# Chunk sizes of the first MLP: six chunks of up to 448 tokens in place of eight of 256 and 320

## The chip, the cores and the metric

The kernel runs on one core of a Trainium2 chip. TensorE (PE) multiplies, VectorE (DVE), ScalarE (ACT) and GpSimd (POOL) do the elementwise work, and the SyncE queue (SP) issues most transfers. Each engine takes its own instructions in order. The metric is the device time of one launch in microseconds; the program computes all of the reference in that launch.

## The reference

Sliding-window attention with 8 heads, then two gated MLPs, all in float32:

```
scores = (q @ k.T) / sqrt(64) - slope[h] * |i - j|      # 4 batches, 8 heads, 576 positions, 64 wide
scores = where(0 <= i - j < 128, scores, -1e9);  attn = softmax(scores);  x = attn @ v
x = x as (2304 tokens, 512)
x = max(max(x @ w1, x @ w2), x @ w3) @ w_out            # first MLP, 768 wide
out = (silu(x @ w_gate) * (x @ w_val)) @ w_out2         # second MLP, 1536 wide
```

## The kernel before

Float32 products are made of three fast matmuls each: a value is split into a rounded head and a remainder, and `mm3` (L124 to L129) adds head by head, head by remainder and remainder by head. The splitting is elementwise work: ACT copies (L112, L276, L285), DVE and POOL subtract (L90, `low`).

**Attention.** A unit (`Unit`, L289) is one block of 128 queries (64 at the end of a batch) of one pair of heads; there are 80. It has four steps: `st_scores` (two to four matmuls, then mask, bias and minimum on DVE at L319 and L324, exp on ACT at L329), `st_normalise`, `st_transpose` (two PE transposes at L361, split, two selects on POOL at L377) and `st_values` (probability times value, L391 or L405, and the split of the result into the MLP's input tile `x`). The steps of neighbouring units are staggered by the lags LN, LT, LV = 1, 2, 4. Units are grouped in pieces (b, s): s = 0 holds a batch's queries 0 to 255, s = 1 its queries 256 to 575. The first three pieces, (0,0), (0,1) and (1,0), are `native`: their operands aren't split, and a matmul of theirs appears as two records. For the others `prep_head` (L272) splits each head's queries and keys when a piece begins (tiles `r`, `kl`), and `prep_v` the values.

**First MLP.** A chunk is a piece's tokens: eight chunks, alternately 256 and 320. `up_groups` has 18 groups of 12 matmuls (6 blocks of the width, 3 weights); the first result is copied by ACT (L168), the other two are joined by a maximum on DVE (L170), and POOL splits the block into `h` (L93, L90). `down_groups` has 72 matmuls; ACT copies the four results to `y` (L197, two buffers) and issues the store to `y_dram` on its own queue. The results of both go through four PSUM banks (`ps_m`, L84). Scores have two banks, transposes one, probability times value one (`ps_v`, L215). The 18 weight tiles of the up products are unpacked from 64-bit words and split (`prep_up`, `single`: L101 on ACT, L104, L105, L107 and L90 on DVE), while the first pieces of attention and the first chunk run.

**Second MLP.** `second` (L502) prepares weights (`prep`: `gates`, `values`, `mixed`, `outs`) and tokens in passes of four blocks and then runs products (L621 to L623) and down products (L701 to L703) for 36 steps.

**Order.** `spread` (L487) deals the pieces of side work among the groups of the main work in program order: up(0) with the weights and the second half of piece 1, up(1) with piece 2, and so on; the last chunk is overlapped with the first 25 pieces of the second MLP's preparation (L752 to L755). A scheduler then fixes the order on each engine by its own timeline. Within it, evictions of PSUM have a high priority (HIGH).

Of the kernel before, what the change touches and what calls it, by code (L numbers as in the profile page):

```python
# [20 lines left out]
P = 128  # L21
# [3 lines left out]
SUBS = ((0, 256), (256, 320))  # L25
KEY0 = (0, 128)
KEYN = (256, 512)
BLOCKS = ((0, 1), (2, 3, 4))
# [15 lines left out]
HIGH, EARLY, LAST = 100, 3, 9  # L44
NORM = "aa"
A2, A3 = 4, 2
# [11 lines left out]
def kernel(ctx: ExitStack, tc, q0, k0, q1, k1, qk0, qk1, vv, w123, wo1, wgv, wo2, out):  # L58
# [20 lines left out]
    wraw = em("wraw", 2)  # L79
    hp = em("hp", 2 * NF1)  # L80
    xp = em("xp")
    tmp = em("tmp", 2)
    dram = en("dram", space=bass.MemoryType.DRAM)
    ps_m = en("ps_m", 4, space=PSUM)  # L84
# [63 lines left out]
    def prep_down(k):  # L148
        wo[k] = down_tile(f"wo_{k}")
        for i in range(2):  # L150
            src = wo1[k * P:(k + 1) * P, i * 256:i * 256 + 256]
            raw = words(src, wraw, "wr", 256) if i else words(src, tmp, "y", 256)
            prep_w(raw, wo[k][:, :, i * 256:i * 256 + 256], rest=nc.gpsimd)

    def up_groups(b, s):

        n = SUBS[s][1]
        m = {}

        def group(f, e):  # L160
            xt = x_t[b, s]
# [17 lines left out]
    def down_groups(b, s):  # L179
        t0, n = SUBS[s]  # L180
        t0 += b * S

        def part(ps, d, ks):
            for k in ks:
                ht = hs[b, s, k]
                mm3(ps[:, :n], wo[k], d * P, ht[:, 0, :], ht[:, 1, :], k == 0, k == NF1 - 1)

        def group(ds):
# [13 lines left out]
    order = [(b, s) for b in range(B) for s in range(2)]  # L202
# [11 lines left out]
    ps_t = ea("ps_t", 1, space=PSUM)  # L214
    ps_v = ea("ps_v", 1, space=PSUM)  # L215
# [3 lines left out]
    fill = att.tile([P, 1, 32], F32, name="fill")[:, :, :1]  # L219
# [4 lines left out]
    def load_first(s, p):  # L224

        nq, nk = SUBS[s][1], KEYN[s]
        c0, nkb = KEY0[s] // P, nk // P
        q = hp.tile([P, 2, nq], F32, tag=f"h{s}", name="qz", bufs=NF1)
        if s == 0:
            if p % 2 == 0:  # L230
                first["k", p] = first["k", p + 1] = qkr.tile([P, 832], F32, tag="qkr", name="kn")
                first["v", p] = first["v", p + 1] = vp.tile([P, 2, 2, 2, P], F32, tag="v", name="vn", bufs=3)
            k, v = first["k", p][:, p % 2 * nk:], first["v", p][:, p % 2, 0]
        else:
            k = prep.tile([P, 832], F32, tag="r", name="kn")
            if p % 2:
                v = vp.tile([P, 4, P], F32, tag="rv", name="vn")
            else:
                v = vp.tile([P, 4, 2, P], F32, tag="v", name="vn", bufs=3)[:, :, 0]
        nc.sync.dma_start(out=k[:, :nk], in_=(k0, k1)[s][0, p])  # L240
        nc.sync.dma_start(out=q, in_=(q0, q1)[s][0, p])
        if s == 0 and p % 2 == 0:
            nc.sync.dma_start(out=first["v", p][:, :, 0], in_=vv[0, p:p + 2, :, c0:c0 + nkb].rearrange("b p k d -> p b k d"))
# [45 lines left out]
    class Unit:  # L289


        def __init__(u, b, s, p, j):
# [3 lines left out]
            u.kb = j - 1 - KEY0[s] // P  # L296
# [576 lines left out]
```

## Time and profile before

| | |
|---|---|
| median of 3 runs | 862.67 us (861.38 to 863.37) |
| the profiled execution | 863.15 us, its span 861.4 us |
| PE, weight loads, DVE, ACT, POOL busy | 98%, 92%, 68%, 49%, 44% of the span |
| mean granted clock of PE | 0.994 of full speed |
| matmuls of the first MLP | 1152 of 256 columns and 1152 of 320 |

Busy time of PE counts matmuls that overlap, so the pace of a stage is read from the starts of neighbouring matmuls in the timeline, not from their durations. A window row gives, for a stretch of the span, the busy time and number of instructions of each engine, then the granted clock, the share of the DMA engines, and GB/s.

### The profile page before, as it was taken

To read this page: it belongs to the slowest core of one execution; us is meant where nothing else is said; L and a number is where in the kernel's file an instruction comes from. 1 tells how busy PE (TensorE), PEld (TensorE's weight loads), DVE (VectorE), ACT (ScalarE), POOL (GpSimd) and SP (SyncE) were. 2 spreads that over 40 slices of the span, in tenths; PEclk is the share of its full clock that TensorE was granted. 3 is DMA by queue.
4 is the path that set the end of the run, shared out by engine and by line. 5 is a ranking of instruction groups with operands and counts; after the bars stand their busy time and mean duration, and the time that the engine had idled before them with its cause. 6 is when DMAs were issued, how large, how long until landed. Compare 5 with 4: busy or idle time off the path is not lost.

```text
span 861.4 us, 15755 instructions
## 1 busy us (share of the span) xinstructions
PE 847.5 (98%) x5352; PEld 791.9 (92%) x5352; DVE 588.4 (68%) x1551; ACT 426.0 (49%) x1182; POOL 382.2 (44%) x555
## 2 busy tenths in 40 slices
PE   8998999999999999999999999999999999999998
PEld 5687999999999999999989999999999999999996
DVE  7998956766678675646979989995564844433342
ACT  6976747847577575624446555543422422221220
POOL 5576867766777677563433231221421221211110
PEclk9998999999999999999999999999999999999999
DMA  9841614324222231302368686914939322736322
GB/s 330 308 151 57 186 44 133 92 72 129 65 73 76 94 113 34 128 2 60 138 209 296 202 309 236 327 64 138 333 138 314 123 80 74 263 128 223 132 74 97
DMA packets 59088, 130.26 MB, mean 151 GB/s; under 512 B 6272, under 2 KB 17536, under 8 KB 59008
## 3 DMA queue, kind: packets, MB, share of 16 engines
q1 hardware_dynamic: 54400, 124.54, 42.9%
q10 hardware_dynamic: 4608, 4.72, 1.6%
q8 instruction: 42, 0.69, 0.3%
q14 instruction: 38, 0.31, 0.1%
HBM read 93.85 MB, written 35.39 MB: 150 GB/s over the span
## 4 chain that ended last, share of the span: by engine, by line
PE 87%; DVE 5%; DMA 4%; ACT 1%; issue 1%; POOL 1%; SPq 0%; DVEq 0%; ACTq 0%; POOLq 0%
PE ps L128 10%; PE ps L127 10%; PE ps L129 10%; PE pg L622 7%; PE pg L623 7%; PE pg L621 7%; PE po L703 6%; PE po L702 6%; PE po L701 6%; PE pc L621 3%; PE pc L622 3%; PE pc L623 3%; PE pv L405 3%; PE pt L361 2%; PE sc L316 1%
## 5 line engine op out<-in xcount | busy, mean ns | idle before, releaser
L90 POOL TENSOR_TENSOR act<-h,act 128x384 fp32r<-128x384 f32 x72 | 80.9, 1144 | 286.1 <-ACT act L112 266.9
L129 PE MATMUL ps<-x,w 128*128 128x320 f32 (+1 forms) x576 | 173.3, 302 | 0.1
L127 PE MATMUL ps<-x,w 128*128 128x320 f32 (+1 forms) x576 | 172.8, 304 | 0.4 <-ACT w L112 0.3
L128 PE MATMUL ps<-x,w 128*128 128x320 f32 (+1 forms) x576 | 172.4, 300 | 0.0
L621 PE MATMUL pg<-ya,u 128*128 128x384 f32 x360 | 121.4, 337 | 1.8 <-ACT y L197 1.8
L622 PE MATMUL pg<-ya,u 128*128 128x384 f32 x360 | 121.6, 338 | 0.0
L623 PE MATMUL pg<-ya,u 128*128 128x384 f32 x360 | 121.2, 337 | 0.0
L127 PEld LDWEIGHTS ps<-x,w 128*128 128x128 f32 x576 | 109.0, 190 | 3.1 <-ACT w L112 1.0
L129 PEld LDWEIGHTS ps<-x,w 128*128 128x128 f32 x576 | 109.5, 190 | 2.5 <-DVE w L90 1.1
L128 PEld LDWEIGHTS ps<-x,w 128*128 128x128 f32 x576 | 109.5, 190 | 1.3 <-issue 0.9
L377 POOL TENSOR_SCALAR_AFFINE_SELECT t<-pk 128x512 fp32r<-128x512 f32 (+3 forms) x128 | 78.3, 634 | 55.2 <-PE pv L405 18.5
L702 PE MATMUL po<-u,act 128*128 128x512 f32 x216 | 85.2, 394 | 0.0
L703 PE MATMUL po<-u,act 128*128 128x512 f32 x216 | 84.6, 395 | 0.0
L701 PE MATMUL po<-u,act 128*128 128x512 f32 x216 | 83.9, 389 | 0.0
L630 DVE TENSOR_TENSOR u<-pg,s 128x384 f32<-128x384 f32 x72 | 39.6, 552 | 60.9 <-PE pg L623 60.7
L329 ACT ACTIVATE z<-z,mn 128x128 f32<-128x128 f32 (+1 forms) x160 | 63.2, 397 | 24.4 <-DVE mn L324 23.8
L621 PEld LDWEIGHTS pg<-ya,u 128*128 128x128 f32 x360 | 68.1, 189 | 6.1 <-ACT y L197 2.4
L622 PEld LDWEIGHTS pg<-ya,u 128*128 128x128 f32 x360 | 68.1, 189 | 4.1
L623 PEld LDWEIGHTS pg<-ya,u 128*128 128x128 f32 x360 | 68.0, 189 | 0.6
L170 DVE TENSOR_TENSOR m<-ps,m 128x256 f32<-128x256 f32 (+1 forms) x96 | 43.1, 450 | 26.9 <-PE ps L129 25.6
L101 ACT ACTIVATE wf<-wr 128x512 f32<-128x512 f32 (+1 forms) x66 | 41.5, 632 | 37.6 <-DMA wr<-wgv 20.9
L352 ACT ACTIVATE z<-z,rc 128x128 f32<-128x128 f32 (+1 forms) x144 | 49.8, 395 | 19.4 <-DVE rc L343 17.9
(115 smaller groups left out, 2051.4 us busy)
## 6 DMA issues: line engine op xcount, KB each, us to landing
ya<-a_dram SPq DMA_DIRECT2D x56, 384.0 KB, 4.8
a_dram<-ya SPq DMA_DIRECT2D x42, 384.0 KB, 5.7
wr<-wgv SPq DMA_DIRECT2D x24, 512.0 KB, 5.2
qkr<-qk SPq DMA_DIRECT2D x24, 416.0 KB, 3.5
wr<-w SPq DMA_DIRECT2D x18, 512.0 KB, 5.9
o_dram<-acc SPq DMA_DIRECT2D x36, 256.0 KB, 2.8
acc<-o_dram SPq DMA_DIRECT2D x36, 256.0 KB, 2.7
wr<-wo SPq DMA_DIRECT2D x12, 512.0 KB, 5.0
```

The lines of the kernel that those rows point to most:

```text
L90: eng.tensor_tensor(out=out, in0=raw, in1=head.bitcast(F32), op=ALU.subtract)
L127: nc.tensor.matmul(ps, wh, xt_h, start=first, stop=False)
L128: nc.tensor.matmul(ps, wh, xt_l, start=False, stop=False)
L129: nc.tensor.matmul(ps, wl, xt_h, start=False, stop=last)
L329: nc.scalar.activation(out=z[:m, a], in_=z[:m, a], func=AF.Exp, scale=-1.0, bias=mn[:m, a:a + 1], accum_out=sm[:m, a:a + 1],)
L377: nc.gpsimd.affine_select(out=t[:, i, :n, :, :m], in_=w[:, :n, :, :m], compare_op=op, fill=0.0, base=0, pattern=[[0, n], [0, 2], [-sign, m ...
L621: nc.tensor.matmul(o, wh, y[:, 0], start=first and k == 0, stop=False, skip_group_check=True)
L622: nc.tensor.matmul(o, wh, y[:, 1], start=False, stop=False, skip_group_check=True)
L623: nc.tensor.matmul(o, wl, y[:, 0], start=False, stop=k == 1, skip_group_check=True)
L701: nc.tensor.matmul(po, ah, w[:, 0], start=j == 0, stop=False)
L702: nc.tensor.matmul(po, ah, w[:, 1], start=False, stop=False)
L703: nc.tensor.matmul(po, al, w[:, 0], start=False, stop=j == PASS - 1)
```

## The change

The chunks of the first MLP no longer follow the pieces of attention. There are six, of 256, 320, 384, 448, 448 and 448 tokens, across the borders of batches, and the pieces are cut so that each chunk is filled by whole pieces: two in batch 0, three in batches 1, 2 and 3. `SUBS` holds them per batch as ranges of blocks, and `span` gives a piece's first query, its queries, first key and keys. Shorter pieces mean more of them: 8 that aren't native in place of 5, so `prep_head` runs 64 times in place of 40, and `prep_v` 32 times in place of 20; the first three pieces are as before. Where a piece has at most 128 queries, DVE subtracts the queries' remainder, not POOL.

The first MLP has three PSUM banks (MB) and probability times value two (VB); the four banks come back for the second MLP (`ps_m2`). `h` has one set of six buffers for the later chunks, not two; the transposed probabilities `t` have three buffers. The side work is dealt out in other shares (A2, A3, LAST), and for the first pass of the second MLP the output weights are prepared after all the others (`late`).

```diff
-SUBS = ((0, 256), (256, 320))
-KEYN = (256, 512)
-BLOCKS = ((0, 1), (2, 3, 4))
+CHUNKS = ((0, 256), (256, 320), (576, 384), (960, 448), (1408, 448), (1856, 448))
+WIDE = 448
+SUBS = (((0, 2), (2, 5)), ((0, 2), (2, 3), (3, 5)), ((0, 2), (2, 3), (3, 5)), ((0, 1), (1, 3), (3, 5)))
+ORDER = [(b, s) for b in range(4) for s in range(len(SUBS[b]))]
+NATIVE = ORDER[:3]
+def span(b, s):
+    j0, j1 = SUBS[b][s]
+    q0, k0 = j0 * 128, max(j0 - 1, 0) * 128
+    return q0, min(j1 * 128, 576) - q0, k0, j1 * 128 - k0
-HIGH, EARLY, LAST = 100, 3, 9
+HIGH, EARLY, LAST = 100, 3, 3
-A2, A3 = 4, 2
+A2, A3 = 8, 5
+QV = 128
+N1, N2 = 21, 25
+MB, TB, VB = 3, 1, 2
...
-    ps_m = en("ps_m", 4, space=PSUM)
+    ps_m = mctx.enter_context(pool("ps_m", MB, space=PSUM, side="right", reuse_waits="tile"))
...
-    def up_groups(b, s):
-        n = SUBS[s][1]
+    def up_groups(c):
+        n = CHUNKS[c][1]
...
-    ps_v = ea("ps_v", 1, space=PSUM)
+    ps_v = ea("ps_v", VB, space=PSUM)
...
-        low(nc.gpsimd, r[D:P, :nq], raw[D:P, :nq], r[D:P, :nq])
+        low(nc.vector if nq <= QV else nc.gpsimd, r[D:P, :nq], raw[D:P, :nq], r[D:P, :nq])
...
-            return [lambda: (load(0), load(1)), gates, values, lambda: (load(2), mixed()), outs]
+            return [lambda: (load(0), load(1)), gates, values, mixed, lambda: load(2), outs]
-        def preps(fs):
+        def preps(fs, late=False):
             todo = [prep(f) for f in fs]
+            if late:
+                out = todo[0][:3] + todo[1][:1]
+                for n, pieces in enumerate(todo):
+                    out += pieces[3:4]
+                    if n + 2 < len(todo):
+                        out += todo[n + 2][:1]
+                    if n + 1 < len(todo):
+                        out += todo[n + 1][1:3]
+                return out + [piece for pieces in todo for piece in pieces[4:]]
...
-    spread(up_groups(0, 1), conv_o, a2[:len(a2) * A2 // 8])
-    spread(down_groups(0, 0) + down_groups(0, 1), a2[len(a2) * A2 // 8:] + a3[:len(a3) * A3 // 8])
-    spread(up_groups(*order[2]), a3[len(a3) * A3 // 8:], early=EARLY)
-    for i in range(3, len(order) - 1):
-        spread(down_groups(*order[i - 1]) + up_groups(*order[i]), attn_units(i + 1), early=EARLY if i + 2 < len(order) else LAST)
+    a2 = attn_units(2) + attn_units(3)
+    a3 = attn_units(4) + attn_units(5)
+    spread(up_groups(1), conv_o, a2[:cut2])
+    spread(down_groups(0) + down_groups(1), a2[cut2:] + a3[:cut3])
+    spread(up_groups(2), a3[cut3:], early=EARLY)
+    spread(down_groups(2) + up_groups(3), attn_units(6) + attn_units(7) + attn_units(8), early=EARLY)
+    spread(down_groups(3) + up_groups(4), attn_units(9) + attn_units(10), early=LAST)
...
-    conv = tokens_steps(0) + preps(range(PASS))
-    spread(down_groups(*order[-2]) + up_groups(*order[-1]), conv[:21])
+    conv = tokens_steps(0) + preps(range(PASS), late=True)
+    spread(down_groups(4) + up_groups(5), conv[:N1])
```

Two places show what the scheduler makes of it. The first is DVE at the end of the first chunk, in the kernel before: `w_5_1` and `w_5_2` are the last two of the 18 weight tiles that up(0) needs, `m` is the maximum of one of its groups, `kl` and `r` are remainders of keys and queries of a piece that isn't native.

```order
L90 TENSOR_TENSOR w_5_1_1272<-wr,w_5_1_1272 128x512
L319 COPY_PREDICATED sc<-later,fill 128x2x128
L104 TENSOR_SCALAR wf<-wf 128x256
L105 SCALAR_TENSOR_TENSOR wf<-wr,wf 128x256
L343 RECIPROCAL rc<-sm 128x2
L107 SCALAR_TENSOR_TENSOR wr<-wr,wf 128x256
L90 TENSOR_TENSOR w_5_2_1336<-wr,w_5_2_1336 128x512
L170 TENSOR_TENSOR m_1313<-ps_1320,m_1313 128x256
```

The same place on DVE now, the last twelve rows up to the same tile:

```order
L336 COPY_PREDICATED sc<-later,sc 128x2x128
L105 TENSOR_TENSOR kl<-qkr,r 128x256
L105 TENSOR_TENSOR r<-qkr,r 64x128
L358 TENSOR_SCALAR sm<-sm 128x2
L105 TENSOR_TENSOR kl<-qkr,r 128x256
L105 TENSOR_TENSOR r<-qkr,r 64x128
L120 SCALAR_TENSOR_TENSOR wf<-wr,wf 128x256
L341 ISA z,mn<-sc,bias 128x128
L341 ISA mn 128x1
L341 ISA z,mn<-sc,bias 128x128
L341 ISA mn 128x1
L105 TENSOR_TENSOR w_5_2_1333<-wr,w_5_2_1333 128x512
```

Between the two tiles there were five instructions, and there are sixteen: scores of later units and key and query remainders of piece (1,1), which before came after this chunk, stand ahead of its last weight tiles.

The second place is ACT at the end of the first MLP, in the kernel before: `y_6904` to `y_6960` are the last results of the last down groups, `u0_4` to `u2_4` and `wf` belong to the second MLP's weights, `s1` is an eviction of its first product.

```order
L198 DMA y_dram_85<-y_6904 128x320
L112 CAST u0_4_6668<-wr_6614 128x512
L101 ACTIVATE wf_6963<-wr_6907 128x512
L112 CAST u1_4_6785<-wr_6732 128x512
L197 COPY y_6930<-ps2_6911 128x320
L112 CAST u2_4_6938<-wr_6850 128x512
L198 DMA y_dram_85<-y_6930 128x320
L197 COPY y_6960<-ps2_6941 128x320
L101 ACTIVATE wf_7005<-wr_6909 128x512
L644 COPY s1_6994<-pg_6987 128x384
```

The same place on ACT now:

```order
L211 COPY y_6381<-ps2_6341 128x448
L212 DMA y_dram_82<-y_6375 128x448
L127 CAST u3_2_6421<-tt_6413 128x512
L212 DMA y_dram_82<-y_6381 128x448
L211 COPY y_6410<-ps2_6391 128x448
L127 CAST u0_4_6490<-wr_6446 128x512
L212 DMA y_dram_82<-y_6410 128x448
L127 CAST u1_4_6524<-wr_6493 128x512
L127 CAST ya_6665<-yr_6578 128x384
L127 CAST ya_6668<-yr_6578 128x384
L211 COPY y_6443<-ps2_6424 128x448
L212 DMA y_dram_82<-y_6443 128x448
```

No unpacking (`wf`) of freshly loaded weights stands between the last four results any more; two casts of the next tokens (`ya`) stand before the fourth.

## Rows read from the trace of the kernel before

**Rows 1.** The page's busy time of each engine.

```profile
PE 847.5 (98%) x5352; PEld 791.9 (92%) x5352; DVE 588.4 (68%) x1551; ACT 426.0 (49%) x1182; POOL 382.2 (44%) x555
```

**Rows 2.** Window of the steady stretch: stretch, length, busy time and count by engine.

```profile
140.00:390.00 250.00, 250.00 (x1940) 247.09 (x1940) 171.64 (x635) 153.18 (x491) 170.86 (x295) 1.00 0.26 80
```

**Rows 3.** Windows of the start, as rows 2.

```profile
50.00:60.00 10.00, 10.00 (x80) 8.35 (x79) 9.14 (x26) 7.85 (x28) 8.37 (x13) 1.00 0.52 154
60.00:70.00 10.00, 9.66 (x85) 8.44 (x84) 8.90 (x24) 6.26 (x22) 8.42 (x11) 1.00 0.36 111
70.00:80.00 10.00, 7.87 (x39) 6.45 (x40) 7.75 (x27) 5.24 (x20) 5.67 (x13) 0.66 0.14 41
80.00:90.00 10.00, 9.87 (x75) 8.61 (x74) 8.80 (x24) 9.28 (x32) 4.73 (x9) 1.00 0.13 43
```

**Rows 4.** Windows of the passage to the second MLP, as rows 2.

```profile
440.00:450.00 10.00, 8.23 (x42) 7.58 (x41) 5.43 (x8) 5.98 (x12) 4.76 (x3) 0.89 0.96 304
450.00:460.00 10.00, 10.00 (x57) 10.00 (x56) 9.78 (x20) 6.00 (x12) 2.15 (x1) 0.94 0.87 276
```

**Rows 5.** PE timeline, 256 columns: start, duration, engine, line.

```profile
374.20 0.28 PE L128 MATMUL ps<-x,w 128*128 128x256 f32 x1
...
377.31 0.28 PE L127 MATMUL ps<-x,w 128*128 128x256 f32 x1
```

**Rows 6.** PE timeline, 320 columns.

```profile
418.75 0.31 PE L127 MATMUL ps<-x,w 128*128 128x320 f32 x1
...
422.57 0.31 PE L129 MATMUL ps<-x,w 128*128 128x320 f32 x1
```

**Rows 7.** PE timeline of the second MLP, 512 and 384 columns.

```profile
500.51 0.39 PE L701 MATMUL po<-u,act 128*128 128x512 f32 x1
...
501.67 0.34 PE L621 MATMUL pg<-ya,u 128*128 128x384 f32 x1
...
505.05 0.33 PE L621 MATMUL pc<-ya,u 128*128 128x384 f32 x1
...
506.96 0.33 PE L623 MATMUL pg<-ya,u 128*128 128x384 f32 x1
```

**Rows 8.** PE waits of the passage, 440 to 470 us: total, times, longest.

```profile
PE pg L621 <- ACT y L197: 1.8, 2, 1.1
```

**Rows 9.** ACT timeline of the passage; in brackets the idle time before.

```profile
444.22 0.66 ACT L101 ACTIVATE wf<-wr 128x512 f32<-128x512 f32 x1 [2.74 <-DMA wr<-wgv]
...
445.32 0.43 ACT L197 COPY y<-ps 128x320 f32<-128x320 f32 x1
...
447.30 0.42 ACT L197 COPY y<-ps 128x320 f32<-128x320 f32 x1 [0.98 <-DMA y_dram<-y]
```

**Rows 10.** DVE groups by form: count, busy us, mean ns, idle before.

```profile
L324 DVE CUSTOM_DVE_ANT_0 z<-sc,bias 128x128 f32<-128x128 f32 x128 | 32.0, 282 | 1.0
...
L319 DVE COPY_PREDICATED sc<-later,sc 128x256 f32<-128x256 int16 x48 | 20.0, 417 | 10.1 <-PE sc L316 8.0 <-PE sc L311 1.6
...
L90 DVE TENSOR_TENSOR kl<-qkr,r 128x256 fp32r<-128x256 f32 x16 | 10.1, 652 | 1.1 <-ACT r L276 1.0
```

**Rows 11.** DVE timeline at the end of the first chunk.

```profile
90.30 0.28 DVE L324 CUSTOM_DVE_ANT_0 z<-sc,bias 128x128 f32<-128x128 f32 x1
...
90.51 0.28 DVE L324 CUSTOM_DVE_ANT_0 z<-sc,bias 128x128 f32<-128x128 f32 x1
...
91.05 0.41 DVE L170 TENSOR_TENSOR m<-ps,m 128x256 f32<-128x256 f32 x1
```

**Rows 12.** PE timeline of native attention.

```profile
66.16 1.47 PE L311 MATMUL sc<-qkn 128*128 128x256 f32 x8
67.47 0.38 PE L361 MATMUL pt<-ident,z 128*128 128x128 f32 x2
...
68.76 0.28 PE L129 MATMUL ps<-x,w 128*128 128x256 f32 x1
68.97 0.67 PE L391 MATMUL pv<-t,vn 128*64 128x128 f32 x8
```

More of the change, by code (lines that the diff above doesn't have):

```diff
@@ L57, with kernel @@
 @with_exitstack
-def kernel(ctx: ExitStack, tc, q0, k0, q1, k1, qk0, qk1, vv, w123, wo1, wgv, wo2, out):
+def kernel(ctx: ExitStack, tc, q0, k0, q1, k1, *rest):
+    qks, (vv, w123, wo1, wgv, wo2, out) = rest[:-6], rest[-6:]
+    qks = dict(zip([u for u in ORDER if u not in NATIVE], qks))
     nc = tc.nc
@@ L200, in down_groups @@
         return [lambda ds=ds: group(ds) for ds in ((0, 1), (2,), (3,))]
-    order = [(b, s) for b in range(B) for s in range(2)]
     actx = ExitStack()
@@ L242, in load_first @@
         if s == 0 and p % 2 == 0:
[L243 removed]
+            nc.sync.dma_start(out=first["v", p], in_=vv[0, p:p + 2, :, c0:c0 + nkb].rearrange("b p k d -> p b k d"))
         elif s:
@@ L295, in __init__ @@
             u.k0 = P if j == 0 else 0
-            u.kb = j - 1 - KEY0[s] // P
-            u.q0 = j * P - SUBS[s][0]
+            q0, u.nq, k0, _ = span(b, s)
+            u.kb = j - 1 - k0 // P
+            u.q0 = j * P - q0
     pairs = {}
     def st_scores(u):
-        nq = SUBS[u.s][1]
+        nq = u.nq
         sc = ps_s.tile([P, 2, 256], F32, tag="sc", name="sc")
@@ L418, in x_part @@
         m = u.mq
-        n = SUBS[u.s][1]
-        if (u.b, u.s) not in x_t:
-            t = xp.tile([P, NP, 2, n], F32R, tag=f"x{u.s}", name=f"x{u.s}")
-            x_t[u.b, u.s] = [t[:, p] for p in range(NP)]
-        return x_t[u.b, u.s][u.p][:, :, u.q0:u.q0 + m]
+        t0 = u.b * S + u.j * P
+        c = max(i for i in range(len(CHUNKS)) if CHUNKS[i][0] <= t0)
+        t0 -= CHUNKS[c][0]
+        if c not in x_t:
+            t = xp.tile([P, NP, 2, CHUNKS[c][1]], F32R, tag=f"x{c % 2}", name="x")
+            x_t[c] = [t[:, p] for p in range(NP)]
+        return x_t[c][u.p][:, :, t0:t0 + m]
     def split_x(u, xr):
@@ L429, in split_x @@
         low(nc.gpsimd, xt[:, 1], xr[:, :m], xt[:, 0])
-    units = [Unit(b, s, p, j) for b, s in order for p in range(NP) for j in BLOCKS[s]]
-    todo = [(b, s, p) for b, s in order for p in range(NP)]
+    units = [Unit(b, s, p, j) for b, s in ORDER for p in range(NP) for j in range(*SUBS[b][s])]
+    todo = [(b, s, p) for b, s in ORDER for p in range(NP)]
     raws = {}
@@ L443, in prep_next @@
             b, s, p = todo[i]
-            pairs[b, s, p] = heads if native(b, s) else [prep_head(s, r) for r in heads]
-            pairs[b, s, p].append(rv if native(b, s) else prep_v(s, rv))
+            pairs[b, s, p] = heads if native(b, s) else [prep_head(b, s, r) for r in heads]
+            pairs[b, s, p].append(rv if native(b, s) else prep_v(b, s, rv))
     def begin():
@@ L553, in preps @@
                 more = todo[n + 1] if n + 1 < len(todo) else []
-                out += pieces[3:4] + more[:1] + pieces[4:] + more[1:3]
+                out += [lambda a=pieces[3], b=pieces[4]: (b(), a())] + more[:1] + pieces[5:] + more[1:3]
             return out
@@ L750 @@
     preps, keep, tokens_steps, tokens_again, head, middle, tail, down = second(apool, raws2, ps_o)
-    conv = tokens_steps(0) + preps(range(PASS))
-    spread(down_groups(*order[-2]) + up_groups(*order[-1]), conv[:21])
-    spread(down_groups(*order[-1]), conv[21:25])
-    conv = conv[25:]
+    conv = tokens_steps(0) + preps(range(PASS), late=True)
+    spread(down_groups(4) + up_groups(5), conv[:N1])
+    spread(down_groups(5), conv[N1:N2])
+    conv = conv[N2:]
     mctx.close()
+    ps_m = em("ps_m2", 4, space=PSUM)
     temp = em("temp")
@@ L847 @@
         "k1": c(kt[:1, ..., 128:640].reshape(1, NP, P, 512)),
-        "qk0": twice(np.concatenate([qt[..., 0:256], kt[..., 0:256]], axis=-1)),
-        "qk1": twice(np.concatenate([qt[..., 256:576], kt[..., 128:640]], axis=-1)),
+        **{
+            f"qk{b}{s}": twice(np.concatenate([qt[b:b + 1, ..., q:q + m], kt[b:b + 1, ..., k:k + n]], axis=-1))[0]
+            for b, s in ORDER if (b, s) not in NATIVE for q, m, k, n in [span(b, s)]
+        },
         "vv": c(vpad.reshape(B, NP, 2, 5, P, D).transpose(0, 1, 4, 3, 2, 5).reshape(B, NP, P, 5, P)),
```

97 lines of the change are left out of this document (50 added, 47 removed).

## The prediction, made before the changed kernel had run

> **What bounds the kernel now.** I read the page first: TensorE is busy 98% of the span [rows 1]. Then the windows by stage. From 140 to 390 us PE has no idle time at all, while DVE is busy 172 of 250 us, ACT 153 and POOL 171 [rows 2]; the last column but one says that the transfers take a quarter of the DMA engines. In that stretch only the time of the matmuls themselves counts, and work on the other engines is free as long as it stays within its 30 to 40% of idle time. Two places are different. In the first 90 us PE has gaps and DVE is nearly full: 9.14, 8.90, 7.75 and 8.80 of each 10 us from 50 to 90, and from 70 to 80 the granted clock falls to 0.66 after PE had stood still [rows 3]. And at the passage to the second MLP PE is idle 1.77 of the 10 us from 440, with the clock at 0.89 and 0.94 [rows 4]. So I price three things: the pace of matmuls by width, the start, the passage.
>
> **Pace.** A busy PE row overlaps its neighbours, so I take starts. 256 columns: 26 steps from 374.20 to 377.31, 0.1196 us each [rows 5]. 320: 26 steps from 418.75 to 422.57, 0.1469 [rows 6]. 384: 11 steps from 505.05 to 506.96, 0.1736; 512: 5 steps from 500.51 to 501.67, 0.232 [rows 7]. Every chunk has 216 up and 72 down matmuls, whatever its width. Before, 4 chunks of each width: 1152 x (0.1196 + 0.1469) = 307.0 us. Now 288 x (0.1196 + 0.1469 + 0.1736 + 3 x w), where w is the step of 448 columns, which no row shows. Halfway between 384 and 512 it is 0.2028, and the sum 302.0: **-5.0 us**. By the price per column of the wide rows (0.452 to 0.453 ns) w is 0.2025 to 0.2030; by that of the 320 row (0.459 ns) 0.2057, and the gain 2.5. I keep 2.5 to 5.3 and take 5.0, since the two wide rows enclose 448. The matmuls of attention are as many as before: 80 units, the same three native pieces.
>
> The Trainium skill, TensorE: Matmul & The Clock Gate, Back-to-back issue gap, gives a step of N / 2.4 ns plus about 2.5 ns. By that only the 2.5 ns of the 576 matmuls that go would be won, 1.4 us. It does not agree with the rows here: it makes 109 ns of 256 columns, where the row has 119.6 [rows 5].
>
> **The passage.** PE waited 1.8 us for `y` copies [rows 8]. The rows of ACT show why: the third copy (445.32) stood behind a `wf` (444.22) that had waited 2.74 us for a weight load, and the fourth waited for the store of an earlier `y` [rows 9]. Now no `wf` stands between the last four `y`; the output weights come after them, attention ends earlier against the end of the first MLP (its last value matmuls stand 246 us of first-MLP matmuls after the start in the order, by the steps above, not 259), so DVE has about 10 us more for the second MLP's weights, and a down group of 448 columns lasts 18 x 0.203 = 3.7 us, not 2.6, so a store has longer to free its `y`. What there is to win is 1.77 us of idle time and, at the lower clock, 10 x 0.11 + 10 x 0.06 = 1.7 [rows 4], together 3.5. I take **-3.2** and leave 0.3 for the cast of the next tokens ahead of the fourth `y`, which waits for its load. Ends: 0, if another load takes the blocking place, and -3.5.
>
> **The start.** Here the scheduler's order costs something. Counted in the order of DVE up to the last maximum of up(0) (at 91.05 before [rows 11]), there are more instructions now: 10 bias-and-minimum, 5 masks, 8 key remainders of 256 columns, 2 of 384, 8 query remainders on 64 partitions, 9 tiny ones on two columns; one key remainder of 512 and three unpackings of 256 columns fewer. Neighbours on DVE overlap by 0.07 us: an instruction of 0.28 has a successor after 0.21 [rows 11]. With durations less 0.07 [rows 10]: 10 x 0.21 = 2.1; 5 x 0.35 = 1.7; 8 x 0.58 = 4.6; 2 x 0.7 (between one and one and a half times 0.652, less the overlap) = 1.4; the 8 query remainders, an operation DVE did not do, at no more than 0.21 = 1.7; 9 x 0.12 (an estimate: about half the 0.21 of a longer one) = 1.1; less 4 x 0.58 = 2.3. Together 10.3 us more DVE work ahead of the end of the first chunk. PE has more to do up to there as well: 17 score matmuls of split pieces (256 columns, 0.12) 2.0; 2 native ones (8 records, four instructions, in 1.31 us [rows 12]) 0.7; 10 transposes, at most 0.12 each, 1.2; 10 native value matmuls (8 records, four instructions, 0.67) 1.7; six up(1) matmuls fewer, 0.9. That is 4.7, work that is only earlier, not more. If DVE is the bound, the surplus 10.3 - 4.7 = 5.6 is lost, since PE has no idle time later in which an earlier attention would pay. But DVE had 0.86 + 1.10 + 2.25 + 1.20 = 5.4 us idle from 50 to 90 [rows 3], and the second bank for values and the third buffer of `t` let units run further ahead into it. I take half of that: 5.6 - 2.7 = **+2.9**. Ends: 0.2, and 5.6 for full DVE; and 3.4 us (10 x (1 - 0.66) [rows 3]) either way for the clock, which fell after the gap there and may fall once more or not at all.
>
> PE enters native value matmuls from other work 8 times more often in the new order (42, not 34), as one now often stands alone between matmuls of the chunk. An entry has a step of 0.21 (68.76 to 68.97 [rows 12]) in place of 0.12; with the way back, which I bound by 0 and the same 0.09, 0.7 to 1.4: **+1.0**.
>
> **What costs nothing.** Splitting more pieces adds 24 casts and 12 value casts on ACT, 24 key and 24 query remainders on DVE; a part of that is in the start's sum, the rest is spread over 250 us in which DVE idles 78 and ACT 97 [rows 2]. POOL gets fewer columns of queries. Maxima and copies have fewer instructions on more columns. SP issues 24 transfers more, smaller ones, and the value and key loads of piece (1,1) now pass the last loads of the down weights, which are wanted only after up(1); a quarter of the DMA engines is in use there. Three banks for `ps_m`: an eviction may now be two groups late, not three, before PE waits: 2 x 12 x 0.12 = 2.9 us in up(0), 4.9 us with 448 columns, against 0.41 for a maximum [rows 11]. That cover is gone only if DVE or ACT has 3 us of other work queued ahead of it, as can be in the start; it belongs to the slow rival below.
>
> **Sum.** -5.0 - 3.2 + 2.9 + 1.0 = -4.3. The profiled execution took 863.15 (span 861.4), so 858.85; the median of the runs is 0.48 lower, which gives **858.4 us**.
>
> **Rivals.** (a) The start isn't slowed: DVE takes the earlier work into its idle time and the gap around 70 us with its low clock goes. For it: DVE's largest idle time lies just there, and units wait less for value banks. Against: DVE is over 88% busy in the three other windows. -5.0 - 3.2 - 3.4 + 1.0 = -10.6: 852.1. (b) The passage isn't mended: something else stands in front of a `y` (the `ya` casts wait for loads that wait for buffers). For it: the DMA share there is 0.96 [rows 4]. -5.0 + 2.9 + 1.0: 861.6. (c) Width saves only a fixed cost of the matmuls that go: 320 columns lie 0.1469 - 320 x 0.4525 = 2.1 ns above the wide rows' price, and 576 x 2.1 ns = 1.2, so -1.2 - 3.2 + 3.9 = -0.5: 862.2. The 256 column row, 3.8 ns above that price, speaks against it. This is the case that the rule of the Trainium skill, TensorE: Matmul & The Clock Gate, leads to. (d) Slower: at the end of the first chunk DVE's queue becomes what PE waits for. The surplus of 5.6 is lost in full, with three banks PE stalls on maxima behind key remainders as well, and the clock falls a second time (3.4), with 1.4 for the entries: 5.6 + 3.4 + 1.4 = 10.4 against -5.0 - 3.2: +2.2, 864.9. It decides once the start loses more than 8.2 us; for it speaks DVE's order, against it that the clock fell only once in 90 us so far.
>
> **Chances.** The forecast, taken from 855 to 860.9: 0.48. (a) 0.22. (b) 0.12 and (c) 0.06, both within 0.2%, which is 861.0 to 864.4 and about what a measurement of this kernel can tell from no change. (d) 0.12. So faster 0.70, same 0.18, slower 0.12. The range takes in (a), (b), (c) and the middle of (d): 851 to 865. The forecast's own range is 855 to 861.
>
> **What would show it.** Steps near 0.203 between matmuls of 448 columns; under 0.5 us of idle PE and a clock of 1.00 between the last down group and the first products; the last maximum of up(0) on DVE at 96 to 100 us; PE without idle time from there to the passage. I am wrong if 448 columns take 0.206 or more, if the start ends within 2 us of where it did, or if PE waits anywhere in the middle.

## The result: slower, and the profile after

The changed kernel takes **872.3 us** (median of four runs), the kernel before 862.0 beside it. One of the four, the profiled one, ran at a clock of 0.85 from end to end and took 923.5 us, so the ratio, 1.011 (95% interval 1.0077 to 1.0143), is of the other three (869.8 to 873.1), and the profile shown is of a second set. That set gave 871.31 against 862.78: 1.0102 (1.0078 to 1.0126); its profiled run has a span of 870.9 us. 858.4 was predicted, and faster.

The page's busy times of the kernel after, against [rows 1]: PE's busy time hardly differs, with 576 matmuls fewer, and its idle time is 7.8 us longer of the 9.5 by which the spans differ.

```profile
PE 849.2 (98%) x4776; PEld 775.9 (89%) x4776; DVE 601.1 (69%) x1575; ACT 430.9 (49%) x1198; POOL 380.2 (44%) x543
```

The pace, from PE's timeline of the kernel after: seven steps of 448 columns, from the first row here to the second, take 1.42 us, 0.203 each (start, duration, engine, line).

```profile
329.83 0.37 PE L142 MATMUL ps<-x,w 128*128 128x448 f32 x1
...
331.25 0.36 PE L143 MATMUL ps<-x,w 128*128 128x448 f32 x1
```

The windows of the kernel after, in the columns of [rows 3], and the steady stretch of [rows 2]. From 50 to 100 us PE is now idle 1.27 + 0.05 + 1.70 + 2.03 + 0.84 = 5.9 us, before 2.6; DVE is over 90% busy in four of the five. The granted clock is 0.83 in two windows, where it was 0.66 in one before: either way 10 us x 0.34 = 3.4 us, so the clock is no part of the difference here.

```profile
50.00:60.00 10.00, 8.73 (x68) 6.70 (x67) 9.62 (x30) 9.09 (x35) 6.80 (x11) 1.00 0.47 147
60.00:70.00 10.00, 9.95 (x75) 7.92 (x76) 8.52 (x30) 8.40 (x31) 7.66 (x17) 1.00 0.56 179
70.00:80.00 10.00, 8.30 (x63) 6.57 (x61) 9.86 (x32) 9.80 (x34) 4.42 (x9) 1.00 0.34 106
80.00:90.00 10.00, 7.97 (x44) 6.87 (x44) 9.79 (x30) 7.81 (x28) 3.98 (x6) 0.83 0.26 81
90.00:100.00 10.00, 9.16 (x57) 9.16 (x58) 9.17 (x34) 7.50 (x24) 3.03 (x5) 0.83 0.36 100
140.00:390.00 250.00, 248.07 (x1489) 233.65 (x1488) 172.91 (x630) 155.71 (x497) 165.08 (x286) 1.00 0.30 92
```

DVE's timeline of the kernel after at the last maximum of up(0), which answers to [rows 11]: it stands at 98.42, 7.4 us later, with a mask, a reciprocal and a key remainder of attention in front of it.

```profile
97.29 0.42 DVE L336 COPY_PREDICATED sc<-later,sc 128x256 f32<-128x256 int16 x1
97.62 0.16 DVE L360 RECIPROCAL rc<-sm 128x2 f32<-128x2 f32 x1
97.70 0.80 DVE L105 TENSOR_TENSOR kl<-qkr,r 128x384 fp32r<-128x384 f32 x1
98.42 0.41 DVE L185 TENSOR_TENSOR m<-ps,m 128x256 f32<-128x256 f32 x1
```

The passage, in windows of the kernel after ([rows 4]). The first MLP ends at 445.6; behind it PE is idle 2.79 and 2.13 us of 10, before 1.77 of 10 once.

```profile
440.00:450.00 10.00, 9.87 (x52) 9.14 (x51) 7.05 (x11) 5.48 (x11) 3.85 (x2) 1.00 0.75 237
450.00:460.00 10.00, 7.21 (x40) 6.57 (x40) 5.79 (x11) 3.55 (x6) 1.32 (x2) 1.00 0.30 102
460.00:470.00 10.00, 7.87 (x36) 7.55 (x36) 6.41 (x13) 4.44 (x9) 1.81 (x2) 0.83 0.95 344
```

What PE waits for there and in the end of the attention, 379 to 625 us (total, times, longest). No `y` copy is among it, as [rows 8] had it; the second MLP's own evictions have taken its place.

```profile
PE pg L649 <- ACT s L672: 2.1, 1, 2.1
PE pg L649 <- ACT h L701: 1.7, 2, 1.6
PE ps L142 <- POOL x L108: 1.6, 1, 1.6
PE pg L649 <- DVE u L658: 1.4, 2, 1.2
PE pc L649 <- DVE u L658: 1.2, 2, 0.8
PE ps L142 <- POOL h L108: 0.8, 1, 0.8
```

ACT's timeline says why ([rows 9]; in brackets the idle time before). The last two `y` copies, shown here, wait for nothing but PE and for the casts of the next tokens ahead of the fourth. But two `wf`, for output weights, hold the queue for 4.85 and 3.03 us until their loads arrive, and an `h` (with a table load of 1.28 us ahead of it) and the `s` that PE waits for stand behind them.

```profile
445.00 0.53 ACT L211 COPY y<-ps 128x448 f32<-128x448 f32 x1 [1.99 <-PE ps L144]
445.42 0.65 ACT L127 CAST u<-wr 128x512 fp32r<-128x512 f32 x1
...
448.28 0.52 ACT L211 COPY y<-ps 128x448 f32<-128x448 f32 x1
449.20 0.86 ACT L672 COPY s<-pg 128x384 f32<-128x384 f32 x2 [0.40 <-ACT y L211]
454.91 0.66 ACT L116 ACTIVATE wf<-wr 128x512 f32<-128x512 f32 x1 [4.85 <-DMA wr<-wo]
455.59 1.28 ACT L701 ACT_TABLE_LOAD   x1
456.89 0.49 ACT L701 ACTIVATE h<-pg 128x384 f32<-128x384 f32 x1
457.59 0.66 ACT L127 CAST u<-wr 128x512 fp32r<-128x512 f32 x1 [0.22 <-DVE wr L122]
...
463.98 0.66 ACT L116 ACTIVATE wf<-wr 128x512 f32<-128x512 f32 x1 [3.03 <-DMA wr<-wo]
464.54 0.46 ACT L672 COPY s<-pg 128x384 f32<-128x384 f32 x1
```

The first load was issued only at 450.04 (SP's timeline), just after POOL's two splits had freed raw buffers (POOL's timeline, 446.15 + 3.86 = 450.01). POOL had waited for the cast at 445.42, and that one stood behind a `y` copy that waited for PE. There are five raw buffers. The second load is the end of the same chain: the row of SP merges two issues, and the second, at 459.66, comes just after POOL's next split (458.33 + 1.30 = 459.63), which waited for the cast at 457.59, and that one stood behind the first `wf`. So the first wait brought on the second.

```profile
450.04 9.96 SPq L151 DMA_DIRECT2D wr<-wo  x2
```

```profile
446.15 3.86 POOL L105 TENSOR_TENSOR u<-wr,u 128x512 fp32r<-128x512 f32 x2 [7.96 <-ACT u L127]
458.33 1.30 POOL L105 TENSOR_TENSOR u<-wr,u 128x512 fp32r<-128x512 f32 x1 [8.31 <-ACT u L127]
```

**Where the time went.** For each stage I summed PE's steps from matmul to matmul and took off, for each, the step of its shape where nothing waits (0.120, 0.147, 0.174, 0.203, 0.231 for 256 to 512 columns, and so on). Those undisturbed steps come to 809.0 us before and 803.7 after. What is left is the loss:

| loss in us | before | after | difference | predicted |
|---|---|---|---|---|
| undisturbed steps | 809.0 | 803.7 | -5.3 | -5.0 |
| start, to the end of up(1) | 30.0 | 35.4 | +5.4 | +2.9 and +1.0 |
| attention, to 8 us before its end | 11.0 | 10.3 | -0.7 | 0 |
| from there to 6 us before the end of the first MLP | 0.1 | 3.7 | +3.6 | 0 |
| passage, the next 51 us | 4.7 | 8.2 | +3.5 | -3.2 |
| the 135 us after it | 0.7 | 3.3 | +2.6 | 0 |
| the rest | 0.7 | 0.7 | 0 | 0 |

The differences sum to +9.1, the spans differ by 9.5.

Each column is one profile. A second profile of the changed kernel's order of instructions (a_last9, below) has, by the same sum, about 36.5 in the start, 6.2 in the passage and 2.7 behind it; in it the clock stayed whole at the passage, while it fell there in both profiles of the table, for 1.7 us each (0.83 in one window of 10 us after, 0.89 and 0.94 in two before). So a row is good to 1 or 2 us.

### The profile page after: what moved, and what is told of

Same layout as the page of the kernel before. It is cut to its first block, busy times and chain, and to the rows that moved or that the text cites. A ratio compares the mean times of both kernels' runs of the same rounds, so it can differ in the third digit from the quotient of the medians.

```text
span 921.8 us, 14687 instructions
## 1 busy us (share of the span) xinstructions
PE 908.0 (98%) x4776; PEld 813.7 (88%) x4776; DVE 608.3 (66%) x1575; ACT 433.7 (47%) x1198; POOL 374.7 (41%) x543
## 4 chain that ended last, share of the span: by engine, by line
PE 92%; DMA 2%; POOL 1%; DVE 1%; ACT 1%; issue 1%; SPq 0%; DVEq 0%; POOLq 0%; ACTq 0%
PE ps L142 12%; PE ps L143 12%; PE ps L144 12%; PE pg L649 7%; PE pg L651 7%; PE pg L650 7%; PE po L731 6%; PE po L730 6%; PE po L729 6%; PE pc L649 3%; PE pc L651 3%; PE pc L650 3%; PE pv L422 2%; PE sc L328 2%; PE pt L378 2%; PE pv L408 2%
## 5 line engine op out<-in xcount | busy, mean ns | idle before, releaser
L142 PE MATMUL ps<-x,w 128*128 128x448 f32 (+3 forms) x432 | 155.6, 364 | 2.7 <-POOL x L108 1.6
L144 PE MATMUL ps<-x,w 128*128 128x448 f32 (+3 forms) x432 | 156.3, 363 | 0.6 <-DVE w L105 0.6
L143 PE MATMUL ps<-x,w 128*128 128x448 f32 (+3 forms) x432 | 155.3, 360 | 0.0
L649 PE MATMUL pg<-ya,u 128*128 128x384 f32 x360 | 127.9, 356 | 1.2 <-ACT s L672 1.2
L650 PE MATMUL pg<-ya,u 128*128 128x384 f32 x360 | 127.7, 355 | 0.0
L651 PE MATMUL pg<-ya,u 128*128 128x384 f32 x360 | 127.6, 356 | 0.0
L142 PEld LDWEIGHTS ps<-x,w 128*128 128x128 f32 x432 | 84.1, 196 | 11.8 <-POOL x L108 1.7
L394 POOL TENSOR_SCALAR_AFFINE_SELECT t<-pk 128x512 fp32r<-128x512 f32 (+3 forms) x128 | 73.6, 597 | 44.6 <-DVE pk L105 34.9
L144 PEld LDWEIGHTS ps<-x,w 128*128 128x128 f32 x432 | 84.7, 196 | 7.7 <-DVE w L105 1.0
L143 PEld LDWEIGHTS ps<-x,w 128*128 128x128 f32 x432 | 84.8, 196 | 6.5 <-issue 1.1
L730 PE MATMUL po<-u,act 128*128 128x512 f32 x216 | 90.2, 418 | 0.0
L729 PE MATMUL po<-u,act 128*128 128x512 f32 x216 | 89.9, 417 | 0.0
L731 PE MATMUL po<-u,act 128*128 128x512 f32 x216 | 89.1, 417 | 0.0
L649 PEld LDWEIGHTS pg<-ya,u 128*128 128x128 f32 x360 | 69.4, 193 | 7.1 <-ACT s L672 1.5
L650 PEld LDWEIGHTS pg<-ya,u 128*128 128x128 f32 x360 | 69.6, 193 | 5.7
L651 PEld LDWEIGHTS pg<-ya,u 128*128 128x128 f32 x360 | 69.3, 192 | 1.1
L686 ACT ACTIVATE h<-s 128x384 f32<-128x384 f32 x36 | 18.9, 524 | 85.9 <-DVE s L658 85.1
L341 DVE CUSTOM_DVE_ANT_0 z<-sc,bias 128x128 f32<-128x128 f32 (+1 forms) x160 | 40.0, 283 | 26.1 <-PE pt L378 25.4
```

Source lines behind the costliest of these rows:

```text
L142: nc.tensor.matmul(ps, wh, xt_h, start=first, stop=False)
L143: nc.tensor.matmul(ps, wh, xt_l, start=False, stop=False)
L144: nc.tensor.matmul(ps, wl, xt_h, start=False, stop=last)
L394: nc.gpsimd.affine_select(out=t[:, i, :n, :, :m], in_=w[:, :n, :, :m], compare_op=op, fill=0.0, base=0, pattern=[[0, n], [0, 2], [-sign, m ...
L649: nc.tensor.matmul(o, wh, y[:, 0], start=first and k == 0, stop=False, skip_group_check=True)
L650: nc.tensor.matmul(o, wh, y[:, 1], start=False, stop=False, skip_group_check=True)
```

## The experiments

All are timed beside the kernel before; the ratio is to that. "Loss" means the table's.

**Banks.** The kernel after again, with other PSUM banks, and the kernel before with the new banks.

```diff
-MB, TB, VB = 3, 1, 2
+MB, TB, VB = 3, 1, 1      # a_vb1
+MB, TB, VB = 4, 1, 1      # a_banks41
```

```diff
-    ps_m = en("ps_m", 4, space=PSUM)      # b_banks32, of the kernel before
+    ps_m = en("ps_m", 3, space=PSUM)
-    ps_v = ea("ps_v", 1, space=PSUM)
+    ps_v = ea("ps_v", 2, space=PSUM)
```

> The changed kernel once more, for a profile at the full clock. Theory S (start): DVE carries about 10 us more work ahead of the end of the first chunk, and PE waits for it: the last maximum of up(0) at 100 us or later (91.05 before), idle PE plus lowered clock in the first 125 us at least 10 us above before, and a middle with PE busy 250 of 250 us. Theory B (banks): PE waits for evictions of the three banks (ACT m, DVE m, ACT y) for 5 us or more in the middle. Theory W (width): a matmul of 448 columns has a step of 0.215 us or more instead of 0.203, which would be 10 us.

> The changed kernel with one PSUM bank for probability times value, as before (three for the MLP, one unused). On DVE then 4 key remainders stand ahead of the end of up(0), not 10, and scores of fewer units. Theory S: the start loses less, 862 to 866 us against 871.5. Theory B: one bank fewer makes PE wait more, 872 or slower. Theory W: no change.

> The changed kernel with the banks as before: four for the MLP, one for values. DVE has 6 key remainders ahead of the end of up(0), not 10. Theory S: between the changed kernel and one value bank alone, 864 to 868. Theory B: back to 860 or faster, since the fourth bank is what was missing. Theory W: no change.

> The kernel before with three banks for the MLP and two for values, nothing else changed. DVE has 4 key remainders of 512 columns ahead of the end of up(0), not 1, and scores of 2 to 4 more units. Theory S: the start is longer, 864 to 868 against 862. Theory B: slower by 5 us or more with waits for evictions in the middle. Theory W: 862, no change.

After again: 871.31. One value bank: 878.96 (1.0192, 1.017 to 1.0214). Four and one: 885.53 (1.0271, 1.025 to 1.0292). Before with three and two: 868.61 (1.0073, 1.0048 to 1.0099). The step of 448 columns is 0.203, so a wide step as the cause is out. Too few banks for the MLP aren't the cause either: with one value bank, a fourth of them makes the kernel 6.6 us slower. And with one value bank, as before the change, the kernel is slower than with two, mostly because a loss of 10.3 in the attention becomes 26.0 (three and one) and 22.7 (four and one, which also loses 7.6 more behind the attention). But the start gains: 35.4 becomes 27.2 and 28.2, so for the start the second value bank is a part of the cause. With one value bank the units can't run as far ahead, so less attention gets onto DVE ahead of the first chunk's maxima (274 instructions and 283, after 312), and the clock stays whole there; windows of the one-bank kernel at the start:

```profile
70.00:80.00 10.00, 9.19 (x76) 7.81 (x76) 10.00 (x32) 9.02 (x33) 6.98 (x15) 1.00 0.29 80
80.00:90.00 10.00, 9.53 (x74) 8.41 (x76) 9.76 (x33) 8.05 (x32) 5.28 (x11) 1.00 0.36 114
```

Before with the new banks loses 1.5 more at the start, 4.4 more at the end of the first MLP, 1.6 more behind the passage and 1.3 less at it; it also has three banks, not four, in the second MLP, so it says little of the change itself.

**The order of the output weights; the end of the attention; DVE's query remainders.**

```diff
-    conv = tokens_steps(0) + preps(range(PASS), late=True)
+    conv = tokens_steps(0) + preps(range(PASS))      # a_early
-HIGH, EARLY, LAST = 100, 3, 3
+HIGH, EARLY, LAST = 100, 3, 9      # a_last9
-QV = 128
+QV = 0      # a_qv0; a_three has all three edits
```

> The kernel after with one thing undone: the preps of the output weights stand among the others again (late=True taken away). Theory P (the passage): the late preps moved the loads wr<-wo behind the end of the first MLP, where they wait for raw buffers; ScalarE's queue then stands 4.85 and 3.03 us at its wf for them, ahead of the second MLP's first evictions, and TensorE loses 7.9 us over 445 to 485 us and .97 in the stall at 435.8. Without it the loss there is 3 to 5 us, and the time falls by 4 to 6 us, to 865 to 867.5. Rival (the start is most of it, and the passage only shows what the late end of the last tokens costs): within 1.5 us of 871.3, with the wait at another row of the passage. A second rival: the blocking wf goes back between the evictions of the first MLP's last tokens, and the 4 us come back there: the end of the first MLP later by 2 to 4 us, the time 869 to 872.

> The kernel after with LAST 9 in place of 3: nine groups of the last spread stand behind the last attention step, not three. Theory: the 1.7 us in which TensorE waits at 387 us for GpSimd's last parts of x go, and nothing else moves: 869 to 870, with the end of up(5) 1.5 to 2 us earlier. Rival (attention packed tighter loses more in its middle than the end gives): 871.5 to 875, with the loss over 306 to 388 us above 7 us.

> The kernel after with QV 0 in place of 128: the 24 query remainders of 128 columns are GpSimd's again; VectorE has 295 operations ahead of the last max of up(0), not 312 (before: 264). Theory S (VectorE's queue sets the start): the last max of up(0) 1 to 2.5 us earlier than 98.4, and the time 869 to 870.5. Rival (the start is set by something else, the ScalarE copies or the clock): the last max within 0.7 us of 98.4, the time 871 or, where GpSimd is late with x in the middle, up to 874.

> The three edits together (output weights' preps among the others, LAST 9, QV 0). If passage, end of attention and start are three losses that do not overlap: 862 to 865, level with the kernel before or up to 1 us slower. If one loss is passed on to the next (a tail that absorbs them): 866 to 869.

Early: 875.93 (1.0162, 1.0139 to 1.0185), slower by 4.6 where 4 to 6 less was expected. The theory that `late` by itself costs the passage falls. Its rival holds in part: a wait for a `y` copy is back, and the `s` behind a `wf` is worse. PE's waits of this kernel from 388 to 500 us:

```profile
PE pg L649 <- ACT s L672: 5.0, 1, 5.0
PE pg L649 <- ACT y L211: 2.1, 1, 2.1
```

LAST 9: 871.78 (1.0108, 1.0091 to 1.0126), no change, and the wait for POOL's `x` that it was to remove is still 1.6 us. The edit did nothing: every engine runs the instructions of the kernel after in the same order, the 4776 matmuls of PE among them. So its theory stays untested, and the run tells how far two profiles of one order differ.

QV 0: 868.93 (1.0071, 1.005 to 1.0091). Its last maximum came at 96.4, 2.0 us earlier, but the last matmul of up(1) at 138.3, 0.3 later than in the profile above: DVE's other early work still stands ahead of the weights, and PE waits 2.0 us for a weight's remainder, where it had been 1.1. One pair of profiles is too few here. Up to 400 us five profiles have the order of the kernel after (a_again, a_early, a_last9, a_all_before, a_step1): their last maximum stands at 98.4 to 99.2 and the last matmul of up(1) at 138.0 to 139.2, 138.9 in the mean. Three have QV 0 alone of the edits that reach the start (a_qv0, a_three, a_qv0_all): 95.4 to 96.4, and 137.3 to 138.3, 137.8 in the mean. So QV 0 gains about 1 us at the start. The passage (8.2 to 6.2) shows no gain of its own: a_last9 lost as little there, also at a whole clock. All three: 874.86 (1.0153, 1.0131 to 1.0174): the passage lost 11.0.

**The preps away from the first evictions; the start.**

```diff
-N1, N2 = 21, 25
+N1, N2 = 25, 31      # a_all_before; a_qv0_all has QV = 0 as well
-        others += conv[:3]
-        conv = conv[3:]
+        others += conv[:3] if n else []      # a_step1
+        conv = conv[3:] if n else conv
-    prep = ea("prep", 4)
+    prep = ea("prep", 2)      # with QV = 0: a_qv0_prep2
```

> The kernel after with N1, N2 = 25, 31 in place of 21, 25: the preps of the output weights of the first four blocks all stand ahead of the last y copy, none among the second MLP's first evictions. Theory P2 (the passage is lost where ScalarE's queue stands at a wf whose load was issued only when GpSimd's split freed a raw buffer; with late it is 4.85 and 3.03 us of ScalarE at two of them behind 450 us, without late 2.65): none of these stands behind 450 us, the loss over 445 to 485 us falls from 7.9 to 3 to 5 us, the time to 867 to 869. Rival P3 (the raw buffers only let so many preps through before the end of the first MLP, wherever they stand): the same waits come back between or ahead of the y copies, the end of the first MLP or the first s later by 3 us or more, the time 870 to 874.

> The kernel after with the remaining preps begun at the second step of the second MLP, not at its first (N1, N2 as in after). Theory P2: one of the two waits stays (u1_4, ahead of the first s), the other comes a step later; loss over 445 to 485 us 5 to 7 us, time 869 to 871. Rival P3: nothing changes before 470 us and the later preps are late for the first down products: 871 to 874.

> QV 0 (868.9 by itself) and N1, N2 = 25, 31 together. If the two losses do not overlap: 865 to 867. If QV 0 already took the passage's share (its loss there was 6.1 us, against 7.9): 868 to 869.5.

> QV 0 and two buffers for the heads' high and low parts in place of four: VectorE has 286 operations ahead of the last max of up(0), against 295 (QV 0) and 312 (after). Theory S (VectorE's queue sets the start): the last max at 95 to 96, and the end of up(1) 1 us earlier than the 138.6 of QV 0, if the middle holds: 867.5 to 868.5. Rival (what the start gains, up(1) loses, as QV 0 showed: its last max came 2.0 us earlier and the end of up(1) 0.3 later): end of up(1) at 138.3 to 139.5, and with less room ahead in the middle 869 to 873.

All before: 870.05 (1.0093, 1.0075 to 1.0111), and QV 0 with it 867.73 (1.007, 1.0046 to 1.0094). No `wf` stands between 450 and 470 us any more. PE's waits for an `s` and an `h` on ACT fall from 3.7 us to 0.3, and the loss of the passage from 8.2 (6.2 in a_last9) to 5.4, and from 6.2 to 5.5 with QV 0. So the waiting `wf` did cost there. But PE then waits 2.9 us once for an `s` sum on DVE, which is in the 5.4, and the time falls by only 1.3. ACT's timeline of this kernel:

```profile
447.20 0.68 ACT L116 ACTIVATE wf<-wr 128x512 f32<-128x512 f32 x1 [0.71 <-DMA wr<-wo]
447.79 1.22 ACT L127 CAST u<-wr 128x512 fp32r<-128x512 f32 x2
448.91 0.52 ACT L211 COPY y<-ps 128x448 f32<-128x448 f32 x1
450.82 0.66 ACT L127 CAST u<-wr 128x512 fp32r<-128x512 f32 x1 [1.40 <-DVE wr L122]
451.39 0.86 ACT L672 COPY s<-pg 128x384 f32<-128x384 f32 x2
```

DVE's timeline shows the same pattern once more: the `s` sum stands behind sums of the next tokens (`yr`), the first of which waited 3.45 us for its load.

```profile
459.97 0.96 DVE L614 TENSOR_TENSOR yr<-yr 128x768 f32<-128x768 f32 x1 [3.45 <-DMA yr<-y_dram]
...
462.85 0.55 DVE L658 TENSOR_TENSOR s<-pg,s 128x384 f32<-128x384 f32 x1
```

One step later: 874.69 (1.0147, 1.0131 to 1.0163); the passage loses only 4.7, but the end of the first MLP 7.2. Each time the wait has moved, and no order took it away.

QV 0 with two buffers for the heads' parts: **863.54** (1.0015, 1.0004 to 1.0027), far below the 867.5 to 868.5 expected. The loss of the start is 28.8, not 35.4. The buffers let fewer heads be split ahead of their units; the last maximum comes at 91.9, and the clock doesn't fall in the start, which is up to 3.4 of the 6.6 us. Windows of this kernel:

```profile
70.00:80.00 10.00, 8.07 (x63) 6.62 (x62) 10.00 (x30) 9.46 (x32) 5.65 (x11) 1.00 0.34 102
80.00:90.00 10.00, 9.78 (x69) 8.75 (x70) 10.00 (x33) 9.29 (x31) 6.77 (x11) 1.00 0.28 85
90.00:100.00 10.00, 10.00 (x68) 8.65 (x67) 8.79 (x24) 6.35 (x25) 7.84 (x14) 1.00 0.40 125
```

**Which of the two did it, and is it the change's?** a_prep2 is the kernel after with two such buffers alone, b_prep2 the kernel before with them; a_qv0_prep2_all adds N1, N2 = 25, 31, and a_four LAST 9 to that.

> The kernel after with two buffers for the heads' high and low parts in place of four, and nothing else (QV 128 stays; VectorE has 296 operations ahead of the last max of up(0), of them 6 key and 6 query remainders; after 312, QV 0 with two buffers 286). Theory S2 (the early head preps of the new pieces, on ScalarE and VectorE, make the weights and the last max late and let the clock fall): the last max at 92 to 95 us, no stretch of half clock before 100 us, 865 to 867.5. Rival (only both together are under some limit): last max above 96, a half-clock stretch near 85 us stays, 869 to 871.

> The kernel before with two prep buffers in place of four: 265 operations ahead of the last max of up(0) against 264. Theory S2 (it is the change's new early pieces that the buffers hold back): nothing gained at the start, 861.5 to 863.5, or slower where the middle then waits for heads. Rival (the kernel before has the same loss, its 6.8 us at half clock at 72 us): 857 to 860.

> QV 0, two prep buffers, and N1, N2 = 25, 31. Singly the last took 1.3 off after and 1.2 off QV 0. Additive: 862 to 862.8. If the passage's loss depends on where the preps happen to stand: 862.5 to 866.

> The same with LAST 9 as well, which takes away the 1.6 us wait of TensorE for GpSimd's x at the end of the attention (still there in QV 0 with two buffers); by itself LAST 9 brought nothing, since the end of the first MLP then lost 2.0 us more. If that repeats: as without it, 862 to 863; if the loss there came from the late start: 860 to 861.5.

Two buffers alone: 866.29 (1.0037, 1.0025 to 1.0049), start 31.2, no low clock. So the buffers give some 5 of the 7.8 us, the query remainders the rest. Before with two buffers: 867.93 (1.0059, 1.0043 to 1.0075), though its start gains as well (30.0 to 26.5, no low clock before 100 us): it loses 4.1 at the end of the first MLP and 2.9 after the passage, where it had lost 0.1 and 0.7. Its profile is of one of its fastest runs, 865.2, so the rest of what its median lost isn't located. So the early splitting of heads is a cost of both kernels. The same edit gives the start 3.5 us before and 4.2 after, and in both the stretches of low clock, 3.4 us, are gone; the kernel before had 265 instructions ahead of its last maximum in place of 264, so there it isn't DVE's number of instructions that fell. By this edit the change made the cost 0.7 us larger, no more than two profiles of one order differ by; with the query remainders it is 6.6 us. The last two: 864.53 (1.0016, 1.0 to 1.0032) and 863.57 (1.0016, 1.0002 to 1.003), no better than without their further edits; LAST 9 again leaves every engine's order as it was, so these two are one program. No version was measured that beats the kernel before.

## Why the prediction was wrong

**The pace** was right: -5.0 predicted, -5.3 measured, w = 0.2028 against 0.203. Rival (c), a gain of 1.2, falls with it. The Trainium skill, TensorE: Matmul & The Clock Gate, Back-to-back issue gap, gives N / 2.4 ns plus 2.5 ns as the gap of isolated matmuls at full clock; an estimate from it is 189 ns for 448 columns, and the trace's 203 doesn't agree.

**The passage is the step that failed**: -3.2 was predicted, +3.5 came (+1.5 by the profile of a_last9), a third to a half of the whole miss of 13.9 us and its largest part. "Now no `wf` stands between the last four `y`" was true, and the wait for `y` went from 1.8 us to nothing. But the `wf` weren't gone, they were later in the same queue, still waiting for loads. I had only asked what they delayed in the old place, not what stands behind them in the new one: the first `s` and `h` of the second MLP, for which PE waits just as directly. I also allowed DVE 10 us more for these weights; DVE's time wasn't what they waited for, a raw buffer was. Rival (b) named the cause, "another load takes the blocking place", but priced it at no gain; it cost 1.5 to 3.5 us. That it is the `wf` is shown by the run without any between 450 and 470 us, where PE's waits for ACT's `s` and `h` are gone; what a passage without waits would be worth is not shown, since in each order tried something else was late.

**The end of the first MLP**, +3.6, had no term: "PE without idle time from there to the passage" was what I expected to see. 1.6 us are PE's wait for POOL's last `x`, 0.8 for the last `h`, which the first down group needs; the other 1.2 are not accounted for. "Maxima and copies have fewer instructions on more columns" left out POOL: beside the second MLP's preps its rounding of 448 columns takes 2598 ns, beside attention 581. Groups of POOL in the kernel after, from 145 to 380 us and then from 380 to 446 us, and in the kernel before from 396 to 442 us:

```profile
L108 POOL TENSOR_SCALAR h<-m 128x448 fp32r<-128x448 f32 x12 | 7.0, 581 | 4.6 <-DVE m L185 4.4
```

```profile
L108 POOL TENSOR_SCALAR h<-m 128x448 fp32r<-128x448 f32 x6 | 15.6, 2598 | 21.9 <-DVE m L185 21.9
```

```profile
L93 POOL TENSOR_SCALAR h<-m 128x320 fp32r<-128x320 f32 x6 | 6.8, 1135 | 22.2 <-DVE m L170 22.2
```

That the width makes the last `h` late is argued, not shown: the kernel before with two buffers has chunks of 320, and PE waits there as well (its list for the whole span):

```profile
PE ps L128 <- POOL h L90: 1.6, 1, 1.6
```

**The 135 us after the passage**, +2.6, had no term either: PE waits there for DVE's `u` sums (1.2 us in the list above). With all preps ahead of the passage the loss is 2.1, without `late` 1.7, but 6.5 with all three edits, which also lack `late`; between 1.7 and 6.5 in the kernels with the new chunks, and 2.9 in the kernel before with two buffers. What sets it is open.

**The start** had the right mechanism and too small a size: 3.9 predicted with the entries, 5.4 measured (up to 6.6 in the other profiles of the same order). The last maximum stands at 98.4, within the 96 to 100 that I named, and the sum up to it holds. Windows from the start to the last maximum, before and after:

```profile
0.00:91.05 91.05, 82.64 (x558) 64.63 (x559) 79.10 (x271) 68.48 (x238) 57.21 (x105) 0.96 0.59 203
0.00:98.42 98.42, 89.89 (x598) 71.51 (x599) 88.98 (x318) 80.11 (x283) 55.85 (x112) 0.97 0.60 204
```

DVE has 9.9 us more work (10.3 in the sum) and 2.5 us less idle time (2.7 in the sum). So what is too small is PE's loss beyond that sum, of which only the entries had a term: 1.0, with 42 entries in place of 34, where the trace has 43. What they cost by themselves was not tried. (One count was off, without a price in the prediction: SP issues 36 more loads of queries, keys and values, not 24, as those of values rise by 12.) That work pulled ahead of the first chunk sets the start is shown by taking some of it away, by a value bank (27.2), by two buffers (31.2) or by these and the query remainders (28.8). That DVE's share of it counts is shown by QV 0 alone, and for about 1 us; ACT has 11.6 us more work there too (the windows above), and no run tells the two apart beyond that. The number of instructions alone doesn't measure it: QV 0 took 17 away and gave about 1 us, two buffers 16 and, with the clock whole, 4.2.

Rival (d) had the start at 10.4 and the passage mended; rival (a) didn't come, but two buffers with QV 0 show that its start can nearly be had (28.8, no low clock), and that the time then is 863.5, not 852.1, because the other losses stay.

## What to carry to other kernels

An instruction that waits for a load and is moved out of one engine's critical stretch must be followed to its new place: list what stands behind it there, and what frees the buffer that its load needs. When finer pieces are prepared ahead, look at what they stand in front of; a limit on how far ahead (here two buffers, not four) gave back 5 us, 4.2 of them at the start, more than any other single edit. Look at the tails of the stages that had no term too, here PE's waits for the last `x` and the last `h`. And before an experiment is read, see that its edit changed the order of the instructions; where it didn't, the run only tells how far two runs of one program differ.

## What the runs showed of the hardware that was not expected

POOL and DVE slow each other far more than I had allowed for. In the kernel without `late`, DVE's subtractions on 128x256 start every 1.46 us while POOL has three splits in 4.40 us, 1.47 each, one against one; right after POOL's last they take 0.41. DVE's timeline, then POOL's:

```profile
447.82 1.54 DVE L550 TENSOR_TENSOR tt<-wr,tt 128x256 f32<-128x256 f32 x1
449.28 1.53 DVE L105 TENSOR_TENSOR u<-wr,u 128x256 fp32r<-128x256 f32 x1
450.73 0.41 DVE L550 TENSOR_TENSOR tt<-wr,tt 128x256 f32<-128x256 f32 x1
```

```profile
446.12 4.40 POOL L105 TENSOR_TENSOR u<-wr,u 128x512 fp32r<-128x512 f32 x3 [6.67 <-ACT u L127]
```

The Trainium skill, SBUF — State Buffer, Terms, says that the two share one pair of ports, held for a whole instruction, while the other is blocked and doesn't share. These rows agree with it, and so does POOL's 2598 against 581 ns.
